# Attention between column tiles: the turn of q and k moved one step earlier, directly behind P of the unit in front

## The chip, the cores and the metric

One Trainium2 chip, one core. The metric is the device time of one execution in microseconds (us). Engines are named as the profile names them: PE is TensorE (PEld its weight loads), DVE is VectorE, ACT is ScalarE, POOL is GpSimd, SP is SyncE, which issues the loads.

## The reference

A windowed attention with sinks, whose output becomes the input of a dense feed-forward layer, whose output goes to eight experts by a top-1 router:

```python
# q, k, v: 2 x 8 x 768 x 64; n_sink 4, window 128
keep = is_sink | in_window
scores = np.where(keep, scale * q @ k.T, -1e9)
a = np.exp(scores - scores.max(-1)); a = a / (a.sum(-1) + 1e-09)
x = (a @ v) reshaped to 1536 x 512
x = np.maximum(0.01 * (x @ w_in), x @ w_in) @ w_out      # 512 -> 2048 -> 512
logits = x @ w_gate                                      # 8 experts, top 1, capacity 384
out[i] = gate_w[i] * (relu(x[i] @ w1[e]) @ w2[e])        # 512 -> 1024 -> 512
```

## The kernel before

**The dense layer sets the beat.** It runs over six column blocks of 256 tokens. An iteration of a block multiplies a piece of the hidden layer (hps, L1101), passes it through the leaky relu (on ACT and DVE or POOL: g, gr, gp at L1112 to L1131), and two iterations later multiplies it into y (L1149). Matmuls are split into high and low parts (wh and wl, xth and xtl), so that fp32r products reach fp32 accuracy. In block 0 the weights are also converted: DVE turns the raw words of w_in and w_out into fp32 (L1018, L1022, L1028, "words" below), ACT makes the high part wh (L1046) and POOL the low part wl (L1047).

**Attention runs between these matmuls.** The attention of the two 128-token tiles that the next block needs is spread over the current block. Its unit is (t, g): tile t, four of the eight heads (g is 0 or 1). `RingAttention.pipeline` (L735) writes the work of the units into a list of steps; an iteration of the dense layer takes one step. Units start four steps apart (GROUP). For a unit that starts at step s:

- the turn: q and k of the unit are transposed by four PE transposes into one PSUM tile qps (L565); ACT takes them out as qT (L568) and kTh (L570). `turn_low` makes the low parts on DVE (L587, L591).
- scores at s (L618, four tiles sps); their second half writes, among others, the PSUM buffer that pv of the step before (ops) filled, so it waits until DVE has made xtl (L733) from that. ACT and DVE move the scores to pm (L627, L628), DVE takes the maximum mx (L633).
- exp on ACT at s+1 and s+2 (L641); the sum's reciprocal ri on DVE (L649, L650) and the scaling of pm on POOL (L652) at s+3.
- trans at s+5: P of the unit, four transposes into pps (L676) and one of the sink columns into kps (L680), taken out by ACT (L688, L697) or DVE (L685).
- pv at s+7 (L714), xth on ACT (L722), xtl on DVE (`pv_low`, L733) at s+8.

A step has a list `pre`, run ahead of the iteration's matmuls, and a list `mid`, run between them. In `mid` scores, trans and pv of all units are entered first and the turns last. Of four steps the first holds scores, the second trans of the unit in front, the third the turn of the unit behind, the fourth pv.

**The order is the code's** on PE, ACT, POOL and SP. On DVE it is the code's through block 0; the conversion words are dealt out between the attention work there by a planner that counts them at 0.6 us each. From block 1 on DVE's order is chosen by a scheduler. All attention tiles of PSUM rotate through four buffers. The loads of a tile (natq, natk, natv, L176) are issued on SP, two steps ahead of the start of the unit in front, in a queue with the raw weights (rawi, rawo).

The twenty units of this pipeline run from about 24 to 330 us of the span. The first, (2, 0), has its turn one step ahead of its scores whatever TURN says; the other nineteen go by TURN.

Of the kernel before, what the change touches and what calls it, by code (L numbers as in the profile page):

```python
# [31 lines left out]
GROUP, NORM_AT, TRANS_AT, PV_AT = 4, 3, 5, 7  # L32
SINK = 2
PAIR = 2
TURN = 2
ROUTER = 5
EARLY_OPS = (2, 1, 2, 1, 1, 5)
FIRST_RAW = 2
# [391 lines left out]
class RingAttention(Attention):  # L430
# [304 lines left out]
    def pipeline(self, ts, n_first, first):  # L735
# [10 lines left out]
        def put(where, s, f, *a):  # L746
            where[max(s, 0)].append(lambda: f(*a))
# [25 lines left out]
        for t, g, s in units:  # L773
            if s:
                put(mid, s - (TURN if s > n_first else 1), self.turn, t, g)
            if s > n_first:
                put(pre, s - TURN + 1, self.turn_low, t, g)
            else:
# [1650 lines left out]
```

## Time and profile before

| | us |
|---|---|
| median of 3 runs | 551.14 (551.05 to 551.84) |
| profiled execution | 551.71 |
| its span | 550.0 |
| PE busy | 533.1 (97%) |
| DVE busy | 394.2 (72%) |
| ACT busy | 291.6 (53%) |
| POOL busy | 210.7 (38%) |

The profiled execution holds 1.7 us outside its span. Times below are microseconds from the start of the span. The granted clock is 1.00 in each stretch from 0 to 350 us, the higher of the two levels (2.4 GHz). A row of the timeline gives the start, the busy time, the engine, the line and the tiles, how many instructions, and in brackets how long the engine had been idle and who released it. PE's matmuls overlap: what one costs in a stream is the distance between starts, not the busy time.

### The profile page before, as it was taken

To read this page: it belongs to the slowest core of one execution; us is meant where nothing else is said; L and a number is where in the kernel's file an instruction comes from. 1 tells how busy PE (TensorE), PEld (TensorE's weight loads), DVE (VectorE), ACT (ScalarE), POOL (GpSimd) and SP (SyncE) were. 2 spreads that over 40 slices of the span, in tenths; PEclk is the share of its full clock that TensorE was granted. 3 is DMA by queue.
4 is the path that set the end of the run, shared out by engine and by line. 5 is a ranking of instruction groups with operands and counts; after the bars stand their busy time and mean duration, and the time that the engine had idled before them with its cause. 6 is when DMAs were issued, how large, how long until landed. Compare 5 with 4: busy or idle time off the path is not lost.

```text
span 550.0 us, 11107 instructions
## 1 busy us (share of the span) xinstructions
PE 533.1 (97%) x3653; PEld 457.9 (83%) x3653; DVE 394.2 (72%) x935; ACT 291.6 (53%) x858; POOL 210.7 (38%) x338
## 2 busy tenths in 40 slices
PE   8998999999999999999999999999999999999993
PEld 7777756888888888888888889888798988988782
DVE  5999996657439974898469952394587667838991
ACT  5768647765444454545454433373255545527771
POOL 6567579713525533553444552241110110102120
PEclk9999999999999999999999999999999999999998
DMA  9979873999564022420240037673376876747920
GB/s 226 243 226 283 258 268 99 360 276 324 170 225 116 21 57 66 129 56 22 68 128 28 1 113 237 217 228 124 99 215 214 254 243 191 241 130 227 348 81 7
DMA packets 83668, 93.72 MB, mean 170 GB/s; under 512 B 42963, under 2 KB 51155, under 8 KB 83472
## 3 DMA queue, kind: packets, MB, share of 16 engines
q1 hardware_dynamic: 81680, 87.78, 53.1%
q0 software_dynamic: 1920, 5.13, 2.6%
q8 instruction: 31, 0.51, 0.4%
q14 instruction: 37, 0.30, 0.2%
HBM read 74.10 MB, written 19.83 MB: 171 GB/s over the span
## 4 chain that ended last, share of the span: by engine, by line
PE 69%; DVE 14%; issue 8%; DMA 4%; POOL 2%; ACT 2%; POOLq 0%; ACTq 0%; DVEq 0%
PE y L1149 19%; PE hps L1101 19%; PE ph L1669 9%; PE py L1726 8%; DVE junk L1255 3%; DMA out<-ys,gt 3%; DVE word L1018 3%; PE ops L714 3%; DVE word L1022 2%; PE sps L618 2%; PE py L1732 1%; DVE cvt L1028 1%; DMA rawo<-in_moe_w_out 1%; PE pps L676 1%; DVE pm L628 1%
## 5 line engine op out<-in xcount | busy, mean ns | idle before, releaser
L1149 PE MATMUL y<-wh,gp 128*128 128x512 f32 x344 | 126.3, 408 | 0.2 <-POOL gp L1131 0.2
L1131 POOL TENSOR_TENSOR gp<-g,gp 128x256 fp32r<-128x256 f32 x77 | 68.0, 883 | 147.0 <-ACT gp L1129 124.8
L1101 PE MATMUL hps<-xth,wh 128*128 128x256 f32 x320 | 90.8, 284 | 0.0
L1101 PE MATMUL hps<-xtl,wh 128*128 128x256 f32 x320 | 90.4, 282 | 0.0
L1101 PE MATMUL hps<-xth,wl 128*128 128x256 f32 x320 | 90.0, 281 | 0.0
L1498 DVE TENSOR_TENSOR cw<-craw,cw 128x512 fp32r<-128x512 f32 x128 | 82.6, 690 | 4.4 <-ACT cw L1496 1.9
L1120 DVE TENSOR_TENSOR g<-hps,g 128x256 f32<-128x256 f32 x80 | 33.5, 419 | 60.9 <-ACT g L1119 60.7
L1149 PEld LDWEIGHTS y<-wh,gp 128*128 128x128 f32 x344 | 64.5, 188 | 14.7 <-POOL gp L1131 0.9
L1496 ACT CAST cw<-craw 128x512 fp32r<-128x512 f32 x112 | 63.5, 622 | 17.6 <-PE py L1732 9.2
L1149 PE MATMUL y<-wl,gp 128*128 128x512 f32 x172 | 67.6, 393 | 0.0
L1255 DVE SCALAR_TENSOR_TENSOR junk<-x,rows_of 128x512 f32<-128x512 f32 x48 | 62.9, 1311 | 1.2 <-ACT x L1227 1.0
L1101 PEld LDWEIGHTS hps<-xth,wh 128*128 128x128 f32 x320 | 60.3, 189 | 3.1 <-issue 0.4
L1101 PEld LDWEIGHTS hps<-xtl,wh 128*128 128x128 f32 x320 | 60.2, 188 | 2.7
L1119 ACT ACTIVATE g<-hps 128x256 f32<-128x256 f32 x80 | 30.5, 381 | 59.8 <-PE hps L1101 56.7
L1101 PEld LDWEIGHTS hps<-xth,wl 128*128 128x128 f32 x320 | 60.7, 190 | 0.0
L1726 PE MATMUL py<-cw,ht 128*128 128x512 f32 x216 | 53.7, 400 | 0.2 <-DVE ht L1714 0.2
L1129 ACT CAST gp<-g 128x256 fp32r<-128x256 f32 x80 | 32.7, 409 | 33.1 <-DVE g L1120 31.9
L1669 PEld LDWEIGHTS ph<-xt,cw 128*128 128x128 f32 x396 | 49.5, 189 | 0.7 <-issue 0.3
L1669 PE MATMUL ph<-xt,cw 128*128 128x256 f32 (+3 forms) x396 | 49.8, 287 | 0.1
L1726 PEld LDWEIGHTS py<-cw,ht 128*128 128x128 f32 x216 | 39.7, 188 | 9.4 <-DVE ht L1714 1.0
L1742 POOL DMA_INDIRECT out<-ys,gt x9 | 9.7, 1081 | 92.5 <-DVE ys L1741 92.5
L641 ACT ACTIVATE pm<-pm,mx 128x132 f32<-128x132 f32 (+1 forms) x80 | 31.8, 401 | 25.1 <-DVE mx L633 25.1
(264 smaller groups left out, 1024.6 us busy)
## 6 DMA issues: line engine op xcount, KB each, us to landing
craw<-in_moe_w SPq DMA_DIRECT2D x128, 256.0 KB
rawi<-in_moe_w_in SPq DMA_DIRECT2D x16, 512.0 KB
rawo<-in_moe_w_out SPq DMA_DIRECT2D x16, 512.0 KB
places<-zero SPq DMA_DIRECT2D x24, 257.0 KB
wh<-wscr SPq DMA_DIRECT2D x16, 256.0 KB
wl<-wscr SPq DMA_DIRECT2D x16, 256.0 KB
natv<-in_v SPq DMA_DIRECT2D x12, 256.0 KB
out<-zero SPq DMA_DIRECT2D x12, 256.0 KB
```

The costliest lines, as they stand in the source:

```text
L641: self.nc.scalar.activation(a, a, AF.Exp, bias=mx[:, pr, e:e + 1], accum_out=su[:, pr, e, 0:1])
L1101: nc.tensor.matmul(ps, lhsT=w, rhs=x, start=(n == 0), stop=(n == len(mm) - 1))
L1119: nc.scalar.activation(g, ps, AF.Copy, scale=0.01)
L1120: nc.vector.tensor_tensor(out=g, in0=ps, in1=g, op=ALU.max)
L1129: nc.scalar.copy(gp[:, 0], g)
L1131: eng.tensor_tensor(out=gp[:, 1], in0=g, in1=gp[:, 0].bitcast(F32), op=ALU.subtract)
L1149: nc.tensor.matmul(y, lhsT=l, rhs=r, start=(start and n == 0), stop=(stop and n == len(mm) - 1))
L1255: nc.vector.scalar_tensor_tensor(out=junk, in0=self.x2[ts[n]][:, 0:DM], scalar=1.0, in1=self.rows_of[:, :, e], op0=ALU.mult, op1=ALU.mult, ...
L1496: nc.scalar.copy(h, t)
L1498: eng.tensor_tensor(out=l, in0=t, in1=h.bitcast(F32), op=ALU.subtract)
L1669: nc.tensor.matmul(self.ph[f][:, sl], lhsT=self.w[e, "a", h, k][w][:, f * P:(f + 1) * P], rhs=self.xt[:, a, k, sl], start=(m == 0), stop=( ...
L1726: nc.tensor.matmul(self.py[n], lhsT=x, rhs=w, start=(h == 0 and f == 0 and m == 0), stop=(h == self.NH - 1 and f == self.HF - 1 and m == 2))
```

## The change

`TURN` goes from 2 to 3. It is used twice in `pipeline`: the turn of a unit is entered in `mid` of step s - TURN, and its `turn_low` in `pre` of step s - TURN + 1.

```diff
-TURN = 2
+TURN = 3
```

```python
                put(mid, s - (TURN if s > n_first else 1), self.turn, t, g)
            if s > n_first:
                put(pre, s - TURN + 1, self.turn_low, t, g)
```

So the turn goes from step s-2 to s-3, which is step s'+5 of the unit in front: the step of that unit's trans, and directly behind it in `mid`. The first turn that moves, that of unit (2, 1), has no trans beside it. `turn_low` goes from `pre` of s-1 to `pre` of s-2. No instruction is added or removed; SP's order is the same.

PE in block 0, around the turn of unit (3, 0) (pps and kps are the trans of (2, 0), qps the turn of (3, 0)); lines with + stand only in the order after, lines with - only in the one before:

```order
@@ -122,4 +122,6 @@
 L676 MATMUL pps<-ident,pm 128x128 x4
 L680 MATMUL kps_901<-ident,psk_209 128x128
+L565 MATMUL qps<-ident,natq 128x128 x2
+L565 MATMUL qps<-ident,natk 128x128 x2
 L1101 MATMUL hps<-x0h,wh 128x256 x4
 L1101 MATMUL hps<-x0l,wh 128x256 x4
@@ -128,6 +130,4 @@
 L1101 MATMUL hps<-x0l,wh 128x256 x4
 L1101 MATMUL hps<-x0h,wl 128x256 x4
-L565 MATMUL qps<-ident,natq 128x128 x2
-L565 MATMUL qps<-ident,natk 128x128 x2
```

The four transposes pass 24 matmuls of the dense layer and now stand behind the five of the trans.

ACT at the same place (pt and sp are taken out of the trans of (2, 0), qT and kTh out of the turn of (3, 0)):

```order
@@ -66,4 +66,6 @@
 L688 COPY pt<-pps 128x512 x2
 L697 ACTIVATE sp<-kps_901,of_pair 128x128 x2
+L568 ACTIVATE qT<-qps 128x256
+L570 CAST kTh_129<-qps 128x2x128
 L1112 ACTIVATE gr<-hps 128x256
 L1113 ACTIVATE gr<-hps 128x256
@@ -73,6 +75,4 @@
 L1046 CAST wh<-cvt 128x512
 L641 ACTIVATE pm,su_134<-pm,mx 128x132 x2
-L568 ACTIVATE qT<-qps 128x256
-L570 CAST kTh_129<-qps 128x2x128
```

qT and kTh pass two conversions wh (L1046) and now stand ahead of them.

DVE in block 0, from the words ahead of `turn_low` of (3, 0) to the maximum of its scores, before:

```order
L1028 SCALAR_TENSOR_TENSOR cvt<-rawi,word 128x512
L1028 SCALAR_TENSOR_TENSOR cvt<-rawo,word 128x512
L649 TENSOR_REDUCE ri<-su_134 128x4
L650 RECIPROCAL ri<-ri 128x4
L587 SCALAR_TENSOR_TENSOR qT<-qps,qT 128x256
L591 TENSOR_TENSOR kTl_130<-qps,kTh_129 128x2x128
L1018 TENSOR_SCALAR word<-rawo 128x512 x2
L733 TENSOR_TENSOR xtl<-ops,xth 128x2x128
L1022 SCALAR_TENSOR_TENSOR word<-rawo,word 128x512
L628 COPY_PREDICATED pm<-sel,sps 128x128 x4
L633 TENSOR_REDUCE mx<-pm 128x4
```

and the same stretch after:

```order
L587 SCALAR_TENSOR_TENSOR qT<-qps,qT 128x256
L591 TENSOR_TENSOR kTl_130<-qps,kTh_129 128x2x128
L1022 SCALAR_TENSOR_TENSOR word<-rawo,word 128x512
L649 TENSOR_REDUCE ri<-su_134 128x4
L650 RECIPROCAL ri<-ri 128x4
L1028 SCALAR_TENSOR_TENSOR cvt<-rawi,word 128x512
L1028 SCALAR_TENSOR_TENSOR cvt<-rawo,word 128x512
L1018 TENSOR_SCALAR word<-rawo 128x512
L733 TENSOR_TENSOR xtl<-ops,xth 128x2x128
L1018 TENSOR_SCALAR word<-rawo 128x512
L628 COPY_PREDICATED pm<-sel,sps 128x128 x4
L633 TENSOR_REDUCE mx<-pm 128x4
```

`turn_low` passes three words, ri stands two words earlier in the row, and xtl stands one word earlier.

## Rows read from the trace of the kernel before

**Rows 1.** Windows of 50 us: busy us (count) per engine, clock, DMA share, GB/s.

```profile
50.00:100.00 50.00, 47.85 (x309) 32.08 (x308) 43.10 (x94) 31.94 (x106) 39.00 (x48) 1.00 0.69 222
200.00:250.00 50.00, 50.00 (x371) 44.04 (x370) 37.98 (x90) 23.93 (x85) 26.58 (x31) 1.00 0.31 86
```

**Rows 2.** Timeline of PE, one unit's trans and the next turn, 206 to 211 us.

```profile
206.27 0.28 PE L1101 MATMUL hps<-xth,wl 128*128 128x256 f32 x1
...
207.17 0.40 PE L1149 MATMUL y<-wl,gp 128*128 128x512 f32 x1
207.40 0.63 PE L1149 MATMUL y<-wh,gp 128*128 128x512 f32 x2
...
209.63 0.28 PE L1101 MATMUL hps<-xth,wl 128*128 128x256 f32 x1
209.75 0.38 PE L565 MATMUL qps<-ident,natq 128*128 128x128 f32 x2
...
210.42 0.39 PE L1149 MATMUL y<-wl,gp 128*128 128x512 f32 x1
```

**Rows 3.** The page's groups: POOL's gp; busy us, mean ns, idle before and releaser.

```profile
L1131 POOL TENSOR_TENSOR gp<-g,gp 128x256 fp32r<-128x256 f32 x77 | 68.0, 883 | 147.0 <-ACT gp L1129 124.8
```

**Rows 4.** Timeline of PE in block 0, 47 to 73 us.

```profile
47.16 0.66 PE L676 MATMUL pps<-ident,pm 128*128 128x128 f32 x4 [0.44 <-DVE pm L628]
...
52.02 0.74 PE L1101 MATMUL hps<-x0h,wh 128*128 128x256 f32 x4 [0.79 <-ACT wh L1046]
...
58.73 0.39 PE L618 MATMUL sps<-kTh,qT 64*128 64x264 f32 x1 [0.82 <-DVE xtl L733]
```

**Rows 5.** Timeline of ACT in block 0, 51 to 55 us.

```profile
51.32 0.65 ACT L1046 CAST wh<-cvt 128x512 fp32r<-128x512 f32 x1
...
53.67 0.42 ACT L568 ACTIVATE qT<-qps 128x256 fp32r<-128x256 f32 x1
...
54.19 0.45 ACT L1112 ACTIVATE gr<-hps 128x256 f32<-128x256 f32 x1
```

**Rows 6.** Timeline of DVE in block 0, 56 to 60 us.

```profile
56.42 0.41 DVE L587 SCALAR_TENSOR_TENSOR qT<-qps,qT 128x256 fp32r<-128x256 f32 x1
...
57.07 1.28 DVE L1018 TENSOR_SCALAR word<-rawo 128x512 int32<-128x512 int32 x2
58.26 0.41 DVE L733 TENSOR_TENSOR xtl<-ops,xth 128x256 fp32r<-128x256 f32 x1
...
59.19 0.90 DVE L628 COPY_PREDICATED pm<-sel,sps 128x128 f32<-128x128 int32 x4
```

**Rows 7.** Timeline of ACT: the first two copies of the scores to pm.

```profile
58.32 0.45 ACT L627 COPY pm<-sps 128x132 f32<-128x132 f32 x2
```

**Rows 8.** Timeline of DVE in block 0, 71 to 73 us.

```profile
71.68 0.69 DVE L1018 TENSOR_SCALAR word<-rawo 128x512 int32<-128x512 int32 x1 [0.37 <-DMA rawo<-in_moe_w_out]
72.29 0.41 DVE L733 TENSOR_TENSOR xtl<-ops,xth 128x256 fp32r<-128x256 f32 x1
```

**Rows 9.** Timeline of PE in block 0, the second half of the scores at 72 us.

```profile
72.76 0.51 PE L618 MATMUL sps<-kTl,qT 64*128 64x264 f32 x2
```

**Rows 10.** SP's issues: natq of tile 3, and two rawo loads.

```profile
40.40 1.43 SPq L176 DMA_DIRECT2D natq<-in_q  x1
...
65.62 1.66 SPq L990 DMA_DIRECT2D rawo<-in_moe_w_out  x2
```

**Rows 11.** Timeline of POOL, start of its last chain in block 0.

```profile
82.44 1.07 POOL L652 TENSOR_TENSOR pm<-pm,ri 128x528 f32<-128x528 f32 x1 [2.48 <-DVE ri L650]
```

**Rows 12.** Timeline of DVE in block 3, around an xtl.

```profile
230.61 0.41 DVE L733 TENSOR_TENSOR xtl<-ops,xth 128x256 fp32r<-128x256 f32 x1
230.94 1.13 DVE L1255 SCALAR_TENSOR_TENSOR junk<-x,rows_of 128x512 f32<-128x512 f32 x1
```

**Rows 13.** Timeline of PE, second halves of two units' scores.

```profile
232.29 0.41 PE L618 MATMUL sps<-kTh,qT 64*128 64x264 f32 x4
...
247.01 0.77 PE L618 MATMUL sps<-kTh,qT 64*128 64x264 f32 x4
```

## The prediction

> **What bounds the kernel now.** I read the windows of 50 us first. From 100 us on PE is the bound: in 200 to 250 us it is busy for all of the 50 us, while DVE works 38.0, ACT 23.9 and POOL 26.6 [rows 1]. Between 50 and 100 us, in block 0, PE is busy 47.85 of 50, and DVE is busy for 43.1 and POOL for 39.0 [rows 1]. So a moved instruction can change the time in two ways: by what PE pays for it, in all blocks, and by what it makes late or early in block 0. I then read the waits of PE. They are few, nearly all in block 0; the longest ones in attention's reach are for the converted weights wh (0.79), for xtl (0.82) and for pm (0.44) [rows 4]. I followed each through the timelines of PE, ACT and DVE to what released it. The sum is made against the profiled execution (551.71, its span 550.0), which is 0.57 above the median of 551.14; since I look for a difference only, I add it to the median.
>
> **PE's own price: nothing.** The change removes no instruction, so PE can gain only if nine transposes together cost less than five and four apart. In block 3 the turn stands alone between hps and y. From the last hps in front of it to the second y behind it pass 210.42 - 209.63 = 0.79 [rows 2]. Without the turn it would be one distance of hps (209.75 - 209.63 = 0.12) and one of y (207.40 - 207.17 = 0.23), 0.35. So four transposes cost 0.44, 0.11 each. The same difference over the five of the trans is 207.17 - 206.27 = 0.90, less 0.35 = 0.55, again 0.11 each. A group that stands alone pays nothing for it, and moving it next to another saves 0.00 per unit, over 19 units 0.0.
>
> The Trainium skill, "TensorE: Matmul & The Clock Gate" (Single matmul latency, Back-to-back issue gap), gives a matmul by itself (398 + N) / 2.4 ns, 219 ns at N = 128, and some 81 ns in a sustained stream. If each lone group paid that difference, an estimate by that page would be 0.14 per unit and 2.6 in all; the trace does not bear it out, since the matmuls of the dense layer on either side keep PE in a stream.
>
> **Blocks 1 to 4.** On ACT qT and kTh now stand ahead of gr or gp of the step with trans, and delay them by 54.19 - 53.67 = 0.52 [rows 5]. The gp made there is used two iterations later, and POOL, the next in line, idles 124.8 us in total for it [rows 3], 124.8 / 77 = 1.6 for each gp: that hides it; without that cover it would be 0.5 on PE per unit. On DVE `turn_low` (56.42 to 57.07, 0.65 [rows 6]) goes ahead of words or junk that stood in front of it. Its work is the same, but in two units the order after has one more junk ahead of xtl (1.13 [rows 12]). The xtl at 230.61 is done at 231.02, and the second half of the scores would want it at 232.29 [rows 12, 13]: 1.27 of room against 1.13, so the cost is 0; if the other work ahead of it shifts too, I allow 0.5 each, near half a junk, so 0 to 1.0. In two other units (that of 247.01 is one) the second half already waits: four matmuls take 0.77 where 0.41 is usual [rows 13], 0.36 each; if xtl comes earlier there, -0.7. In the order after, junk still stands ahead of xtl in both. I take 0 for the blocks, with -0.7 and +1.0 as ends.
>
> **Loads.** The turn of unit (3, 0) needs natq a step earlier, at about 47.16 + 5 x 0.11 = 47.7, right behind the trans [rows 4]; the 24 matmuls of the dense layer that it passes are 24 x 0.12 = 2.9 [rows 2]. natq is issued at 40.40 [rows 10]. The nearest load whose landing a wait shows is rawo, twice the size: issued from 65.62 on, DVE is let go at 71.68 [rows 8, 10], 6.1 later. By that natq lands by 46.5, 1.2 ahead of the need. Cost 0; if it is late, its lateness, up to some 1 us, on PE. The loads of later tiles stand further ahead of their turns in SP's queue.
>
> **Block 0, step by step.** Here five turns move.
>
> 1. Unit (2, 1): qT and kTh on ACT go into a stretch where ACT waits for DVE's words, so wh behind them comes up to 0.5 earlier. PE gets ahead, until the trans at 47.16 waits for DVE's pm [rows 4], and DVE, back to back with words there, does the same work. Gain 0.
> 2. Unit (3, 0): qT and kTh now stand ahead of two wh. The first starts at 51.32 [rows 5] and PE waits for it until 52.02 [rows 4]; it starts 0.52 later, and so does PE: +0.52, up to the start of its scores.
> 3. The second half of those scores waits for xtl at 58.73 [rows 4]. DVE now has xtl one word earlier, behind one of the two L1018 that take 57.07 to 58.26 [rows 6], so 0.60 earlier, at 57.66. PE goes on at about 58.1, 0.6 earlier than before: step 2 is paid back from a wait that was there anyway, and PE is 0.6 ahead.
> 4. In exchange DVE reaches pm (L628) one word earlier, at 58.6 instead of 59.19 [rows 6], and finds ACT's copies, which started at 58.32 [rows 7] and now start at about 58.5 to 58.8: a wait of 0 to 0.45 on the engine that is full in this block.
> 5. PE keeps the 0.6 to the next scores. Their second half waits for xtl (72.29 [rows 8]), and PE goes on at 72.76 [rows 9]. On DVE the timeline shows one idle time from 56 to there, 0.37 for rawo at 71.68 [rows 8]. That load was issued at 65.62 [rows 10], when DVE's words freed its buffer; with `turn_low` ahead of those words (0.65) and the 0.45 of step 4, it is issued up to 1.1 later, and DVE goes on 0 to 0.45 later. So the 0.6 of PE ends in a longer wait, and what remains is DVE's delay: 0 to +0.45.
> 6. The rest of the block goes by DVE's ri, which starts POOL's chain at 82.44 [rows 11]; POOL then works without a gap to the end of the block. PE gets the delay of step 5 as it is. The last two turns move ACT's work only where POOL is late anyway.
>
> Sum: 0.0 (PE) + 0 (later blocks) + 0.3 (block 0, from 0 to 0.45, nearer to the upper end because each step above hands the delay on) = +0.3, so 551.4. The ends by the bounds are 0 - 0.7 = -0.7 and 0.45 + 1.0 + 1.0 (loads) = +2.5.
>
> **Rivals.**
>
> *Slower, by ACT in block 0.* The 0.52 of step 2 is not paid back: each of the five turns holds wh up, and PE, DVE's pm copies and POOL's wl pass it on. For it: PE does wait for wh there (52.02 [rows 4]), and ACT works in the order of the code. Against it: PE meets a wait for DVE behind each (47.16, 58.73, 72.76 [rows 4, 9]), which takes the delay in. It decides once the delay of wh is longer than these waits, that is if xtl does not come earlier in step 3. Price: 5 x 0.52 = 2.6, 553.7. With the loads and the junk as smaller causes of the same sign I give it 0.20.
>
> *Faster, by the waits of the block.* The 0.6 of step 3 stays, because the rawo load is not what decides at 71.68 and xtl comes earlier there too, and the two later waits of 0.36 go: -0.6 - 0.7 = -1.3, 549.8. For it: the waits are there to be had. Against it: DVE's work up to the wait is the same, and POOL's chain behind it starts from DVE. 0.12.
>
> *Faster, by standing together.* One transpose lasts 0.38 - 0.11 = 0.27 [rows 2], the most that a lone group could pay is 0.27 - 0.11 = 0.16, 19 x 0.16 = 3.0, 548.1. The two differences above say 0.00. 0.04. The page named above would make it 2.6, 548.5.
>
> *Nothing moves.* The order could absorb it all: 551.1. It is the same case as the forecast within what can be told.
>
> **How the numbers follow.** About 0.2%, 1.1 us, is what a measurement of this kernel can tell from no change. Forecast and "nothing moves" together 0.64 (the +0.3 and all that lies within 1.1), slower 0.20, faster 0.12 + 0.04 = 0.16. The range goes from the faster rival (549.8) to near the slower one's price: 549.8 to 553.5; outside lie the gain by standing together (0.04), a part of the other faster case (0.04) and the upper half of the slower one (0.1).
>
> **What would show it.** Right: trans and turn together take nine times 0.11, 0.99, in block 3; the hps wait at 52.02 goes to about 52.5, that at 58.73 to about 58.1; xtl of 72.29 stays or comes up to 0.45 later; PE stays busy 50.0 of 50 in 200 to 250 us. Wrong: a stretch in 100 to 330 us that is shorter by 0.1 per unit (the groups do cost apart); an idle of PE ahead of the turn with the release by natq (loads); waits of PE for wh in all five turns (the slower rival); xtl at 71.7 or earlier (the faster one).

## The result: 0.8% slower, and where the profile after shows it

The changed kernel takes 555.71 us (median of 6 runs, 555.09 to 556.71), the one before 551.1 beside it: the ratio is 1.0079 (95% interval 1.0069 to 1.0089). The profiled execution took 555.65 us, its span 553.8; before they were 551.71 and 550.0.

PE does the same work: 532.7 us busy against 533.1. So 3.8 us of waits were added to the span. I compared the starts of each unit's scores (L618), trans (L676) and pv (L714) with those of before. The difference is flat but for four places: +0.96 in block 0 (from 75 us on), +0.7 between 188 and 203, +1.1 at 250 and +1.1 at 310; behind 328 us it is the 3.8 of the span. The windows of the kernel after show the same (columns as in [rows 1], where 200 to 250 had 50.00):

```profile
50.00:100.00 50.00, 46.62 (x302) 31.22 (x302) 41.98 (x90) 30.92 (x101) 38.10 (x45) 1.00 0.68 213
150.00:200.00 50.00, 49.45 (x357) 43.41 (x355) 38.16 (x95) 24.18 (x89) 19.01 (x22) 1.00 0.38 115
200.00:250.00 50.00, 49.09 (x375) 43.23 (x373) 36.48 (x86) 23.85 (x86) 23.86 (x29) 1.00 0.29 80
300.00:350.00 50.00, 48.87 (x353) 43.49 (x353) 29.91 (x81) 19.44 (x65) 20.38 (x25) 1.00 0.35 109
```

The granted clock is 1.00 in these windows, as in all others up to 350 us of both kernels, so nothing here is a slower PE. The list of PE's waits of the kernel after (total, times, longest) names whom it waits for:

```profile
PE sps L618 <- DVE xtl L733: 3.3, 3, 1.1
PE hps L1101 <- ACT wh L1046: 2.2, 2, 1.3
...
PE pps L676 <- DVE pm L628: 1.0, 1, 1.0
...
PE pps L1317 <- DVE roh L1298: 0.5, 1, 0.5
...
PE y L1149 <- POOL gp L1131: 0.2, 1, 0.2
```

xtl stands at the head, with three waits of about 1.1: one in block 0, one at 250 and one at 310. The roh (the router's one-hot) is the wait at 198; just ahead of it, at 188, the scores take 1.03 from the first start to the last, 0.73 before.

**PE around a turn in block 3**, timeline after, against [rows 2]:

```profile
208.04 0.28 PE L1101 MATMUL hps<-xth,wl 128*128 128x256 f32 x1
208.16 0.60 PE L676 MATMUL pps<-ident,pm 128*128 128x128 f32 x4
208.60 0.27 PE L680 MATMUL kps<-ident,psk 128*128 128x128 f32 x1
208.71 0.38 PE L565 MATMUL qps<-ident,natq 128*128 128x128 f32 x2
208.92 0.38 PE L565 MATMUL qps<-ident,natk 128*128 128x128 f32 x2
209.06 0.48 PE L1149 MATMUL y<-wh,gp 128*128 128x512 f32 x1
209.38 0.40 PE L1149 MATMUL y<-wl,gp 128*128 128x512 f32 x1
```

From the last hps to the second y pass 1.34; less the 0.35 that lies there without a transpose, 0.99 for nine, 0.11 each. Standing together neither gains nor costs anything.

**Block 0**, timeline of PE after, against [rows 4, 9]:

```profile
52.53 0.74 PE L1101 MATMUL hps<-x0h,wh 128*128 128x256 f32 x4 [1.33 <-ACT wh L1046]
...
58.02 0.43 PE L618 MATMUL sps<-kTh,qT 64*128 64x264 f32 x4
...
61.59 0.60 PE L676 MATMUL pps<-ident,pm 128*128 128x128 f32 x4
...
63.22 3.70 PE L1149 MATMUL y<-cvt,gr 128*128 128x512 f32 x8 [0.48 <-DVE cvt L1028]
...
73.72 0.38 PE L618 MATMUL sps<-kTh,qT 64*128 64x264 f32 x1 [1.03 <-DVE xtl L733]
```

and DVE, against [rows 6, 8]:

```profile
57.59 0.41 DVE L733 TENSOR_TENSOR xtl<-ops,xth 128x256 fp32r<-128x256 f32 x1
57.92 0.68 DVE L1018 TENSOR_SCALAR word<-rawo 128x512 int32<-128x512 int32 x1
59.14 0.90 DVE L628 COPY_PREDICATED pm<-sel,sps 128x128 f32<-128x128 int32 x4 [0.54 <-ACT pm L627]
...
72.65 0.69 DVE L1018 TENSOR_SCALAR word<-rawo 128x512 int32<-128x512 int32 x1 [0.80 <-DMA rawo<-in_moe_w_out]
73.25 0.41 DVE L733 TENSOR_TENSOR xtl<-ops,xth 128x256 fp32r<-128x256 f32 x1
```

and SP's issue of that load, against [rows 10]:

```profile
66.83 1.57 SPq L990 DMA_DIRECT2D rawo<-in_moe_w_out  x2
```

PE waits for wh until 52.53, gets xtl earlier and needs no wait at 58.0, and is 0.66 ahead at the trans (62.26 before). It doesn't keep the lead: the next y waits until 63.22 for a cvt of DVE, and at pv PE is 0.08 late (66.85, 66.77 before). DVE waits 0.54 ahead of pm, and `turn_low` of (3, 1), 0.66 with its two rows, now stands ahead of two words; the rawo load behind them is issued 1.21 later (65.62 before). DVE goes on 0.97 later (71.68 before), and PE's wait there grows until it is 0.96 late (72.76 before). How much of the 0.97 comes from the later issue is taken up in experiment 9.

**Blocks 2 to 4.** At 250 and 310 the second half of a unit's scores waits (PE after, against [rows 13]):

```profile
250.23 0.39 PE L618 MATMUL sps<-kTh,qT 64*128 64x264 f32 x1 [1.14 <-DVE xtl L733]
...
310.62 0.39 PE L618 MATMUL sps<-kTh,qT 64*128 64x264 f32 x1 [1.13 <-DVE xtl L733]
```

The reason lies 20 us earlier on DVE. Before, in block 3, ahead of the xtl of [rows 12]:

```profile
226.07 0.39 DVE L1120 TENSOR_TENSOR g<-hps,g 128x256 f32<-128x256 f32 x1
226.38 0.41 DVE L587 SCALAR_TENSOR_TENSOR qT<-qps,qT 128x256 fp32r<-128x256 f32 x1
226.71 0.41 DVE L591 TENSOR_TENSOR kTl<-qps,kTh 128x256 fp32r<-128x256 f32 x1
227.04 1.64 DVE L1255 SCALAR_TENSOR_TENSOR junk<-x,rows_of 128x512 f32<-128x512 f32 x1
...
228.61 0.41 DVE L1120 TENSOR_TENSOR g<-hps,g 128x256 f32<-128x256 f32 x1
228.95 1.72 DVE L1255 SCALAR_TENSOR_TENSOR junk<-x,rows_of 128x512 f32<-128x512 f32 x1
...
246.94 0.41 DVE L733 TENSOR_TENSOR xtl<-ops,xth 128x256 fp32r<-128x256 f32 x1
```

and after:

```profile
228.31 0.39 DVE L1120 TENSOR_TENSOR g<-hps,g 128x256 f32<-128x256 f32 x1
230.09 0.42 DVE L1120 TENSOR_TENSOR g<-hps,g 128x256 f32<-128x256 f32 x1 [1.38 <-ACT g L1119]
230.43 1.62 DVE L1255 SCALAR_TENSOR_TENSOR junk<-x,rows_of 128x512 f32<-128x512 f32 x1
...
232.09 1.18 DVE L1255 SCALAR_TENSOR_TENSOR junk<-x,rows_of 128x512 f32<-128x512 f32 x1
...
233.20 0.42 DVE L733 TENSOR_TENSOR xtl<-ops,xth 128x256 fp32r<-128x256 f32 x1
...
247.87 0.41 DVE L1120 TENSOR_TENSOR g<-hps,g 128x256 f32<-128x256 f32 x1
248.21 1.62 DVE L1255 SCALAR_TENSOR_TENSOR junk<-x,rows_of 128x512 f32<-128x512 f32 x1
...
249.76 0.41 DVE L733 TENSOR_TENSOR xtl<-ops,xth 128x256 fp32r<-128x256 f32 x1
```

DVE's order is a scheduler's here. Before, turn_low and a junk (L1255, one product of the router's logits, whose sum alone is kept) lie between the two g. After, turn_low has gone ahead of everything and both g stand directly behind each other: DVE idles 1.38 for the second. Both junks now stand between it and xtl. Counted from the pt in front (L685), four junks stand ahead of this xtl in both orders, but the hole is new. This xtl itself is in time (PE wants it at 234.01), but DVE has no idle time from there to the next xtl, which comes at 249.76 instead of 246.94, 2.82 later, while PE came to it only 1.7 later. The difference is PE's loss there, and the same pattern stands in block 4.

### The profile page after: what moved, and what is told of

Read it like the earlier page. It is cut to its first block, busy times and chain, and to the rows that moved or that the text cites. A ratio compares the mean times of both kernels' runs of the same rounds, so it can differ in the third digit from the quotient of the medians.

```text
span 553.8 us, 11102 instructions
## 1 busy us (share of the span) xinstructions
PE 532.7 (96%) x3653; PEld 457.8 (83%) x3653; DVE 394.3 (71%) x935; ACT 290.0 (52%) x858; POOL 208.9 (38%) x338
## 4 chain that ended last, share of the span: by engine, by line
PE 46%; issue 19%; DVE 18%; DMA 10%; ACT 3%; POOL 2%; another core or an unknown queue 0%; POOLq 0%; DVEq 0%; ACTq 0%
PE hps L1101 17%; PE y L1149 17%; DMA out<-ys,gt 9%; DVE junk L1255 8%; PE ops L714 2%; PE sps L618 2%; DVE word L1018 2%; DVE word L1022 1%; DVE cvt L1028 1%; DMA rawo<-in_moe_w_out 1%; PE pps L676 1%; DVE pm L628 1%; DVE g L1120 1%; PE py L1726 1%; PE ph L1697 1%
## 5 line engine op out<-in xcount | busy, mean ns | idle before, releaser
L1149 PE MATMUL y<-wh,gp 128*128 128x512 f32 x344 | 124.7, 404 | 0.3 <-POOL gp L1131 0.2
L1131 POOL TENSOR_TENSOR gp<-g,gp 128x256 fp32r<-128x256 f32 x77 | 66.3, 860 | 151.1 <-ACT gp L1129 135.0
L1255 DVE SCALAR_TENSOR_TENSOR junk<-x,rows_of 128x512 f32<-128x512 f32 x48 | 62.3, 1298 | 0.3
```

The lines of the kernel that those rows point to most:

```text
L1131: eng.tensor_tensor(out=gp[:, 1], in0=g, in1=gp[:, 0].bitcast(F32), op=ALU.subtract)
L1149: nc.tensor.matmul(y, lhsT=l, rhs=r, start=(start and n == 0), stop=(stop and n == len(mm) - 1))
L1255: nc.vector.scalar_tensor_tensor(out=junk, in0=self.x2[ts[n]][:, 0:DM], scalar=1.0, in1=self.rows_of[:, :, e], op0=ALU.mult, op1=ALU.mult, ...
```

## The experiments

All comparisons have five rounds; "offset" is the start of a PE group less that of the kernel before, in the profiled executions. The cuts of code are shortened: where DVE keeps the rows of before in block 0, the allowance that the planner counts for a turn also goes back to its old step. In some kernels DVE's rows of blocks 1 to 4 were laid down by hand, with dependencies that fix the order and add no wait.

**1. DVE's rows of before.** PE, ACT and SP in the order after, DVE word for word in that of before. POOL is as after but for the four short rows of `turn_low` (L594) between 137 and 156 us, which go with it; the offset stays within 0.1 there.

```diff
-                put(pre, s - TURN + 1, self.turn_low, t, g)
+                put(pre, s - 1, self.turn_low, t, g)
+    chain(tc)      # DVE, blocks 1 to 4: the rows of before
```

> The turns stand where the change puts them on PE and ACT; DVE's instructions keep the order of the kernel before, row for row, in block 0 and in blocks 1 to 4. Theory (DVE's order makes the loss: turn_low ahead of words and junk makes a rawo load and four xtl late): back to 551.1, within 0.5, no wait of PE for xtl above 0.4 between 100 and 330 us. Rival (ACT makes it: qT and kTh ahead of wh and gp): stays at 554 to 556.

Measured: 552.15, ratio 1.0012 (1.0003 to 1.0021), span 550.8; that is 0.5 above the upper end of the theory (551.6). By the ratios 0.7 us is left of 4.4, so the new order of PE and ACT is not what costs most of it. What is left in the offsets is +0.48 in block 0, +0.44 at 188 to 203, and 0.3 at 250 and 310 together. In block 0 the rawo wait is still longer, though the issue (65.86) is only 0.24 later than before:

```profile
72.17 0.69 DVE L1018 TENSOR_SCALAR word<-rawo 128x512 int32<-128x512 int32 x1 [0.64 <-DMA rawo<-in_moe_w_out]
```

**2 and 3. The change in block 0 alone, and in the later blocks alone.**

```diff
-                put(mid, s - (TURN if s > n_first else 1), self.turn, t, g)
+                put(mid, s - ((TURN if t < 5 else 2) if s > n_first else 1), self.turn, t, g)
```

(turn_low likewise; for the later blocks `t >= 5`.)

> TURN is 3 for the five moved turns of block 0 (tiles up to 4), 2 for the others. Theory: only the +1.0 of block 0 (from the rawo load at 71.7) remains, 552.1 (551.8 to 552.5); DVE's idle time for rawo about 0.8 at 72.6 and the second half of the scores at 73.7. Rival (the loss comes per turn, some 0.24 for each of 19): 5 x 0.24 = 1.2, 552.3, which this run alone doesn't tell apart; the next one does.

> TURN is 2 for the turns of block 0 and 3 for the fourteen of blocks 1 to 4. Theory: the +2.9 of blocks 2 to 4 remains, in four places (about 188, 198, 248 and 308 us: 0.2, 0.4, 1.1, 1.1), 554.0 (553.5 to 554.6), block 0 as before. Rival (per turn): 14 x 0.24 = 3.4, spread evenly over 100 to 330 us, 554.5.

Measured: 552.39, 1.0022 (1.0012 to 1.0031), and 554.02, 1.0055 (1.0042 to 1.0068). Block 0 alone gives the offset of +0.97, and then it stays. The later blocks alone give +0.67 at 188 to 203, +1.04 at 250 and +1.1 at 310, flat between: no price for each turn. The parts add up: 1.07 + 2.70 = 3.8 by the medians, against 3.9 between the profiled executions of the full change and of before (4.6 between their medians); by the ratios it is 0.77% of 0.79%. PE's waits of the third kernel hold the xtl again, though block 0 is as before:

```profile
PE sps L618 <- DVE xtl L733: 3.0, 3, 1.1
```

**4. One turn_low put back.** The change in full, with turn_low of unit (3, 1) alone back at s-1, to have the rawo load issued earlier by its 0.66.

```diff
-                put(pre, s - TURN + 1, self.turn_low, t, g)
+                put(pre, s - (1 if (t, g) == (3, 1) else 2), self.turn_low, t, g)
```

> As the changed kernel, but turn_low of unit (3, 1) alone goes back to its old step, behind four words instead of ahead of them; PE, ACT, POOL and SP are untouched. Theory (this turn_low makes the rawo load late by 0.66): the load of 66.8 is issued at about 66.2, DVE waits for it until 72.0 to 72.2 instead of 72.65, the second half of the scores starts at 73.1 to 73.3 instead of 73.7: 0.5 less than the changed kernel, 555.2. Rival (the load is late because of what else is in the queue): DVE goes on at 72.65 all the same, 555.7.

Measured: 555.1, 1.0073 (1.006 to 1.0086). It is 0.6 below the change, which was timed on another occasion, and its profiled execution lost 1.5 us to a rawi load at 46 us, which of the others only the seventh waits for (0.45). Inconclusive.

**5 and 6. turn_low early alone, and the moved junk alone.** Both are the first experiment with one difference in DVE's rows: in the fifth turn_low stands as early as in the order after; in the sixth it stays late, and junk and g stand as after. In block 3, from the first g to xtl:

```
before:      g  turn_low  junk  g  junk  xtl
fifth:       g  junk  g  junk  xtl            (turn_low ahead of it all)
sixth:       g  turn_low  g  junk  junk  xtl
```

> As the run with DVE's rows of before, but in blocks 1 to 4 turn_low (L587, L591) stands as early as in the changed kernel, behind pt; junk, g, ri and xtl keep the order of before. Theory (turn_low itself costs nothing; junk that lost its place ahead of a g leaves DVE waiting): 552.1 (551.5 to 552.7), no wait of DVE for g above 0.5 at 229 and 289 us, waits of PE for xtl up to 0.5. Rival (turn_low ahead of junk makes xtl late by its own 0.65 and more): 553.5 to 554.5.

> The other half: turn_low keeps its place of before behind ri and g; junk, g, ri and xtl stand in blocks 1 to 4 as in the changed kernel (two g ahead of the junk that stood between them). Theory: DVE waits about 0.7 to 1.4 for the second g at 229 and 289 us, and the xtl of 249 and 309 us make PE wait some 0.8 to 1.2: 553.5 to 554.5. Rival (turn_low's place): 552.

Measured: 553.32, 1.0033 (1.002 to 1.0046), and 557.75, 1.0111 (1.0094 to 1.0128). Both are above what I expected. turn_low by itself does cost about 1 us: the offset grows by 1.1 at 188 to 203, and there, in the timeline of the fifth kernel, turn_low at the head of DVE's queue waits for ACT's kTh, and the junks, xtl and roh stand behind it:

```profile
181.19 0.42 DVE L587 SCALAR_TENSOR_TENSOR qT<-qps,qT 128x256 fp32r<-128x256 f32 x1 [0.59 <-ACT kTh L570]
```

The moved junk makes the hole as expected (sixth kernel, DVE):

```profile
229.50 0.42 DVE L1120 TENSOR_TENSOR g<-hps,g 128x256 f32<-128x256 f32 x1 [0.71 <-ACT g L1119]
```

xtl comes at 250 and 312, and PE waits for it 1.7 instead of the 1.1 of the change. The offset then jumps by 3.3 and 3.2, more than the waits. The rest is the granted clock, in the section at the end. So the place of the junk alone is enough for the losses at 250 and 310. At 188 to 203 either alone is enough: the offset of the sixth grows by 1.0 there, that of the fifth by 1.1, that of the first, with neither, by 0.44. The two don't add up: the full change loses 0.7 there, and by the ratios (1.0111 against 1.0079) the sixth is slower than the full change as a whole, so beside the moved junk an early turn_low gives something back. In the profiles the xtl at 232.62 of the sixth is as late against PE as that at 233.20 of the change; what more it loses up to 250 comes in between, where its nine junks take 12.5 in all instead of 11.9. Why they do was not separated.

**7. A word ahead of pm.** The second experiment with one word (L1022) ahead of pm of (3, 0), to fill the wait at 59.14.

```diff
-        self.pace.vector(1.6)
+        self.pace.vector(1.6); (t, g) == (3, 0) and self.pace.word()
```

> As the run with TURN 3 in block 0 only, but one word (L1022) goes ahead of the pm copies (L628) of unit (3, 0), so that DVE has work while it waits for ACT's copies. Theory: DVE's idle time of 0.52 at 59.1 goes, the words of 60 to 67 us run 0.5 earlier, the rawo load is issued at about 66.3 instead of 66.8, and the second half of the scores starts 0.3 to 0.5 earlier: 551.9 to 552.1, against 552.4. Rival (the rawo load lands when the queue lets it): 552.4.

Measured: 552.07, 1.0013 (1.0001 to 1.0024), which can't be told from the second experiment's 552.39 (1.0012 to 1.0031). In its profiled execution DVE waits 1.10 for ACT's copies all the same, after a late rawi load. Inconclusive.

**8. xtl ahead of junk.** The change in full, only DVE's rows edited in blocks 2 to 4: xtl ahead of the junks directly in front of it (by the trace five places), roh ahead of the two pt. Rows of DVE, not code:

```diff
 g
+xtl
 junk
 junk
-xtl
```

> The changed kernel with one edit on DVE: in blocks 2 to 4 xtl goes ahead of the junk directly in front of it (six places), and roh ahead of the two pt. Theory: PE's waits for xtl of 1.4 at 250 and 310 us fall below 0.4, the one of 0.2 at 189 us stays or goes, that for roh falls by 0.3: 2.0 to 2.6 less than the changed kernel, 553.2 to 553.7. Rival (PE would meet the next late result right behind): at least 555.

Measured: 552.35, 1.0019 (1.001 to 1.0028), better than expected. The offset is 0.68 to 0.84 behind block 0 and 0.86 at the end: against the kernel before, nearly nothing is left of the loss of blocks 2 to 4, with turn_low early, both g together, and PE, ACT, POOL and SP as after. The hole is still there (1.39 at 229.32); xtl there even waits for its own input. At 250 and 310 the scores take 1.14 and 1.11 from first to last start, as in the kernel before (1.09 and 1.10). DVE of this kernel:

```profile
229.32 0.42 DVE L1120 TENSOR_TENSOR g<-hps,g 128x256 f32<-128x256 f32 x1 [1.39 <-ACT g L1119]
230.59 0.42 DVE L733 TENSOR_TENSOR xtl<-ops,xth 128x256 fp32r<-128x256 f32 x1 [0.85 <-ACT xth L722]
```

**9. Block 0 with DVE's rows of before.** The turns move in block 0 on PE and ACT alone.

```diff
-                put(mid, s - (TURN if s > n_first else 1), self.turn, t, g)
+                put(mid, s - ((TURN if t < 5 else 2) if s > n_first else 1), self.turn, t, g)
-                put(pre, s - TURN + 1, self.turn_low, t, g)
+                put(pre, s - 1, self.turn_low, t, g)
```

> TURN is 3 in block 0 only, for PE and ACT; DVE keeps the order of the kernel before throughout. Theory (the +1.0 of block 0 comes from DVE's order, its wait for ACT's pm copies and the later rawo load): 551.3 to 551.8 against 552.4 with DVE's order changed too; no wait of DVE at 59 us, the rawo load issued at 65.6 to 65.9. Rival (qT and kTh ahead of wh on ACT cost it): 552.2 to 552.6.

Measured: 552.27, 1.0018 (1.0008 to 1.0029): the rival's range, and in time it can't be told from the second experiment. In the profile the offset is 0.40 to 0.49, half of the second's, and there is no wait at 59. But the rawo load, issued at 65.55, lets DVE go later than before (71.68):

```profile
72.06 0.69 DVE L1018 TENSOR_SCALAR word<-rawo 128x512 int32<-128x512 int32 x1 [0.84 <-DMA rawo<-in_moe_w_out]
```

One execution doesn't tell the share, since this load varies: with all of block 0 as before, DVE waits 0.37 for it in the kernel before and not at all in the third and the tenth (it goes on at 71.20 and 71.18 there). Together the profiles show a direction. With PE and ACT as after and DVE's rows of before (first, fifth, sixth and ninth) the load is issued at 65.55 to 65.86, and DVE goes on at 71.83 to 72.17, later than in all three with block 0 as before. With DVE's rows of after as well (the change, second and eighth) the issue is at 66.82 or 66.83, and DVE goes on at 72.42 to 72.65. So a part of block 0's loss comes with the order of PE and ACT, and not with DVE's; by the times alone it could be all of it. How large the part is, and why a load that is issued at the same time lands later, is open.

**10. The kernel before, with xtl and roh first**, by the edit of the eighth.

> The kernel before with the one edit on DVE that took the waits out of the changed kernel: xtl ahead of the junk directly in front of it and roh ahead of the two pt, in blocks 2 to 4. Theory: the waits of PE of 0.26 at 247 and 307 us and 0.28 at 197 us go, 0.5 to 0.8 less than the kernel before, 550.6. Rival (they are paid elsewhere): 551.4.

Measured: 550.89, 0.9986 (0.9975 to 0.9997), a little faster than both kernels: 0.8 by the ratio, 0.2 by the medians, between theory and rival. The offset falls by 0.25 at the roh and by 0.35 at the wait of 247.01 [rows 13] and at its like at 307, which is what they held. Another 0.4 in the profiled execution (span 548.2) is the rawo load, for which DVE didn't wait; the third experiment's profile has that too, with the same block 0, so it is the load's own variation.

This kernel is also what the eighth has to be set against, since both have the same edit. By the ratios the moved turn then still costs 1.8 us; in the profiles the offsets of the two lie 1.0 apart behind block 0 (0.68 and -0.33 at 173 us) and 2.2 at the end (0.86 and -1.30). So xtl's place makes up for the loss of the later blocks against the kernel before; about 1.2 of what the turns cost there is still paid, some 0.3 each at 175 and 188 and 0.4 each at 250 and 310.

## Why the prediction was wrong, step by step

**PE's own price: right.** 0.99 for nine, 0.11 each; and PE's busy time is the same.

**Blocks 1 to 4: the step that failed.** It took 0, between -0.7 and +1.0; the change showed +2.9, and the later blocks alone made 2.7 of the medians. I set the one junk more that stands directly ahead of xtl in two units (1.13) against a room of 1.27, and that held: PE doesn't wait for the xtl at 233.20. But I took the cost to end there. DVE has no idle time behind it, so the delay goes on to the next xtl, and I did not walk through DVE's new rows to see what each waits for. Two g next to each other are such a place: ACT's g comes at the pace of hps, so the second has to wait, and what had filled that time now stands behind it. For the unit of 247.01 [rows 13] and its like at 307 the step even had "in the order after, junk still stands ahead of xtl in both" and saw at most a gain. Their 0.36 was not only a wait to be had: it showed that they had no room at all, so that each delay on DVE beyond PE's own would be PE's. Experiment 6 shows that the junk's place alone makes the loss at 250 and 310; experiment 8 shows that xtl's place makes up for the loss of the later blocks, though set against experiment 10 not all of what they cost.

**gr and gp behind ACT's turn: right for PE.** PE waits for gp once, 0.2, in the list above.

**Loads (natq): right.** The turn of (3, 0) starts at 47.73, directly behind the trans, without a wait.

**Block 0, steps 1 to 4: right, in mechanism and nearly in size.** hps at 52.53 (predicted 52.5), PE without a wait at 58.0, 0.66 ahead at the trans (0.6); the wait ahead of pm was 0.54, a little outside 0 to 0.45.

**Block 0, step 5: mis-sized.** It gave 0 to 0.45; DVE went on 0.97 later. The issue came 1.21 later, near the 1.1 predicted, but I let only 0.45 of it through, that is the wait of step 4, as if the landing hung on DVE's own delay. The wait before was 0.37, and no row showed slack behind it. How much of the 0.97 came with the issue is not shown: in the ninth kernel DVE goes on 0.38 later with the issue where it was, and the load varies by as much. A premise was wrong too: PE did not keep the 0.6 to the next scores, it had lost it at 63.22 to a cvt of DVE. Step 6 was right: PE took over the delay as it was, and POOL's chain starts at 83.45 instead of 82.44.

**The rivals.** The slower one gave 553.7 by another mechanism, ACT's wh not paid back. It was, at 58; so "slower" had 0.20 mainly for a reason that did not occur, and of the mechanism that did occur it had only "the junk" as a smaller cause, without a price. "By the waits" and "standing together" did not occur; the waits of 0.36 that the former counted on are real, though, and experiment 10 collects them, by a direct edit.

**What stays open.** Why the rawo load lands later for the same issue, and with it the share of PE and ACT in block 0's 1 us; what of the +0.7 at 188 to 203 goes to which moved row; and which rows make the 1.2 that is left between the eighth and the tenth kernel.

## What to carry to other kernels

Where a scheduler sets an engine's order, a one-step move reorders more than the rows it names, and the price can fall due 20 us behind them: list the new order in full, and ask of every row what it waits for and what stands behind it, not only how many rows stand ahead of the one that matters. A consumer that already waits, by however little, marks a place without room; cost each delay on its producer's engine at full price. Put the short row that PE waits for ahead of filler: here that gave back 3.3 of the 4.4 us by the ratios.

## What the runs showed of the hardware

In the sixth kernel PE waited 1.73 for xtl up to 250.23 and was busy for only 0.50 of the 2 us ahead of it, and the granted clock went to the lower level (1.2 GHz) behind it. Windows of 2 us of the sixth kernel, columns as in [rows 1]:

```profile
248.00:250.00 2.00, 0.50 (x7) 0.29 (x5) 2.00 (x6) 1.02 (x4) 1.45 (x3) 1.00 0.00 0
250.00:252.00 2.00, 1.77 (x9) 1.44 (x10) 2.00 (x6) 0.62 (x3) 0.43 (x1) 0.83 0.00 0
252.00:254.00 2.00, 2.00 (x8) 1.71 (x8) 2.00 (x6) 0.23 (x1) 0.74 (x1) 0.50 0.57 131
254.00:256.00 2.00, 2.00 (x16) 2.00 (x16) 1.93 (x7) 1.17 (x6) 0.00 (x0) 0.82 0.00 1
```

In the same stretch of the changed kernel, where the wait is 1.14 and PE is busy for 1.09 of the 2 us, the clock stays at 1.00. In the sixth kernel y's starts lie 0.43 apart instead of 0.23 meanwhile, which is the rest of its jump. By the mean clock it is not the same in every execution: the sixth kernel's runs go from 556.37, with a mean granted clock of 0.996, to 559.06, with 0.989. Of the jump of 3.3 in the offset 1.7 is there when the second half of the scores starts (from 1.1 to 2.8), so the clock cost about 1.5 more.
